# Delta attention with two feed-forward layers: another order of the opening

## The chip, the cores and the metric

The kernel runs on one core of a Trainium2 chip. The metric is device time in microseconds, from launch to the end of the last instruction; several runs of the same program are given by their median. The engines named below are TensorE (PE), VectorE (DVE), ScalarE (ACT), GpSimd (POOL) and SyncE (SP), whose queue issues the DMAs.

## The reference

For 4 batches and 8 heads, a state of 48 x 48 goes through 768 positions by the delta rule: at each position the output is read with q, then the state takes up what v adds to what the state already says of the normalised k, weighted by beta. The result is laid out as 3072 tokens of 384 columns and goes through two feed-forward layers, the first gated (silu), the second with the mish function.

```python
k_n = k / (np.linalg.norm(k, axis=-1, keepdims=True) + 1e-06)
for t in range(S):
    kt, vt, bt = (k_n[:, :, t], v[:, :, t], beta[:, :, t, None])
    y[:, :, t] = np.einsum('bhd,bhde->bhe', q[:, :, t], state)
    v_old = np.einsum('bhde,bhd->bhe', state, kt)
    state = state + bt[:, :, :, None] * np.einsum('bhd,bhe->bhde', kt, vt - v_old)
...
x = x @ w_gate * sigmoid(x @ w_gate) * (x @ w_val) @ w_out
h = x @ w_in;  out = (h * np.tanh(np.log1p(np.exp(h)))) @ w_out
```

## The kernel before

The 768 positions are cut into 24 chunks of 32; three chunks make a step of 384 tokens, and there are eight steps. Within a chunk the recurrence is written as matrix products. A gram of the keys (gram) gives a triangular system of 32 x 32 for each of 24 systems of a step (3 chunks of 8 heads). Its inverse t is found column by column: one instruction multiplies (t_tmp, lines 298 and 366) and one subtracts (t_sys, lines 305 and 373). In the first two steps only the two halves of 16 are solved so, and two small products, the joins (lines 323 and 334), make the missing corner out of them. For a join the solved system has to be turned around: three transpositions on VectorE (lines 311, 312 and 314) write the right half of t, its transposed left half, and the left half of t. Then z = t v (line 413), the output y (lines 392, 445 and 456) and the state's update ds (line 483) follow. In the first step two batches share one matmul of 64 rows, for which some operands are written twice, each copy masked by turn_of: g_wide, t_wide, tT_wide and p_wide.

Beside this TensorE runs the first feed-forward layer on the tokens of the step before: for each of twelve tiles j the products g and v (line 747, nine matmuls each) and then, one tile late, the product x (line 819, nine matmuls). Each of these is a group; a step has 36 of them. The second layer follows when all steps are done.

The weights arrive as 64-bit numbers and are converted on the chip. For a tile of the first layer ScalarE does lines 677 and 679 on raw, VectorE line 700 (f), ScalarE line 716 and VectorE or GpSimd line 720. The tiles of the second layer go back to device memory. The f tiles of the first layer and the raw tiles of the second share two buffers in turn.

Each engine's queue holds the instructions in the order in which the program writes them. Up to the first product of the main loop that order is the table START: a word is a piece of work (ja0 the first half of a join of chunk 0, jb0 its second half, h4 four matmuls that only keep TensorE's clock, P5 five columns of the second step's solve on GpSimd, vs the scaling of v, qw the masked copy of p, b the conversion of a weight tile). A word with > behind it stops after the matmuls; with > ahead of it the rest follows. In the main loop, the attention of the next step and the weight tiles are events with a time in groups, and an event is written out as soon as the groups reach its time. BEGIN says where in a step the attention of step t begins, FILL where the weight tiles of the first layer are converted, LEAD how much earlier they are loaded.

Of the kernel before, what the change touches and what calls it, by code (L numbers as in the profile page):

```python
# [12 lines left out]
AF = mybir.ActivationFunctionType  # L13
ALU = mybir.AluOpType
# [3 lines left out]
NEXT = 1.4  # L18
TURN = 32.6
CHAIN = (0.0, 0.28, 0.58)  # L20
BEGIN = {1:7.8,2:9.5,3:5.5}
STEADY = 4.0
LAST = 33.0
XSAT = (0.1, 1.7, 3.3)
FB = 3
START = """
sq0 sq1 sq2 h12 kq0 kq1 norm kq2 turn0 scale diag s3 wide kq3 s3 kq4 b0 s3 h17 b1 kg5 h10 s6 back0 mr ma ml vs0 clear vs1 vs2 qw0
ja0> h3 >ja0 turn1 jb0> h4 nb >jb0 ns1 z0> >z0 ja1> >ja1 ns1 u0> >u0 jb1> >jb1 ns1 r1> y1 ne >r1 gam1 z1> >z1 scale diag P5 qw1 P4 qw2 P6 ja2> >ja2 u1> d1 >u1 jb2> >jb2 y0 o0> >o0 d1 r2> y2 >r2 d1 z2> >z2 t1 x0> >x0 o1> >o1 t1 >x0 o2> >o2 x1> t1 >x1 >x1 x2> u2> >x2 >x2 d3 done
"""
FILL = (1.2, 2.9)  # L30
W2AT = (4.5, 4.0, 3)
# [4 lines left out]
OPEN = 2  # L36
# [22 lines left out]
def tile_delta_attention_moe_moe(  # L59
# [10 lines left out]
    nc = tc.nc  # L70
    D = 48
    H = k.shape[2] // D
    B, C = 4, 32
# [4 lines left out]
    CH = NCH * H  # L78
    HB = C // 2
# [4 lines left out]
    J1 = w_first.shape[0] // 3  # L84
# [18 lines left out]
    turn_of = const.tile([128, 2], F32, name="turn_of")  # L103
# [70 lines left out]
    tT_nat = lent10[:, 1, 0:C * 32].rearrange("p (a b) -> p a b", b=C)  # L174
# [423 lines left out]
    ev = []  # L598
# [59 lines left out]
    def fetch(u, n=3):  # L658
        if u >= n_prep or quiet and u >= FIRST:
            return  # L660
        open_raw(u)
        for i in range(came_in[u], min(came_in[u] + n, pieces_of(u))):
            src = w_first[3 * u + i] if u < J1 else w_second[2 * (u - J1) + i]
            nc.sync.dma_start(out=raws[u][:, 384 * i:384 * i + 384], in_=src.rearrange("p k f -> p (k f)"))
            came_in[u] += 1

    def conv_begin(u, which=(0, 1)):
        if u >= n_prep:
            return
        fetch(u)  # L670
        raw = raws[u]
        word = raw.bitcast(U32).rearrange("p (f w) -> p f w", w=2)
        top = raw.bitcast(U16).rearrange("p (f w) -> p f w", w=4)

        high = word[:, :, 1].bitcast(F32)
        if 0 in which:
            nc.scalar.activation(out=high, in_=high, func=AF.Prelu, scale=2.0 ** -112, alpha=2.0 ** 32)
        if 1 in which:
            nc.scalar.activation(
                out=word[:, :, 0], in_=top[:, :, 1], func=AF.Identity, scale=2.0 ** -13, bias=floor  # L680
            )
            words_of[u] = word
            begun[0] = max(begun[0], u + 1)
# [22 lines left out]
    def conv_tail(u, n=3):  # L706
        n = min(n, stepped[u] - tailed[u])
        if not n:
            return
        f, first = parts_of[u], tailed[u]  # L710
        if u < J1:
            sl = slice(3 * first, 3 * (first + n))
            if not first:
                w1_open(u)
            f = f[:, 0:1152].rearrange("p (k f) -> p k f", f=128)
            nc.scalar.copy(out=w1h[u][:, sl], in_=f[:, sl])
            for i in range(first, first + n):
                sl = slice(3 * i, 3 * i + 3)
                eng = nc.vector if u < OPEN else nc.gpsimd
                eng.tensor_tensor(out=w1l[u][:, sl], in0=f[:, sl], in1=w1h[u][:, sl], op=ALU.subtract)  # L720
        else:
            for i in range(2):
                nc.sync.dma_start(
                    out=w2d[u - J1][:, 3 * i:3 * i + 3], in_=f[i].rearrange("p (k f) -> p k f", k=3)
                )
        tailed[u] += n
        while ended[0] < n_prep and tailed[ended[0]] == pieces_of(ended[0]):
            ended[0] += 1
# [236 lines left out]

    hold0 = [{} for _ in range(NCH)]

    def widen(out, in_, at_):
        for x in range(2):
            nc.scalar.activation(  # L970
                out=out[:, :, x, at_], in_=in_[:, 0:CH, at_], func=AF.Identity, scale=turn_of[:, x:x + 1]
            )

    words = {
# [11 lines left out]
            )  # L986
            for x in range(2)
        ],
        "mr": lambda n: widen(t_wide, lent_tn, slice(HB, C)),
        "ma": lambda n: widen(tT_wide, tT_nat, slice(0, HB)),  # L990
        "ml": lambda n: [
            nc.gpsimd.tensor_scalar(
                out=t_wide[:, :, x, 0:HB], in0=lent_tn[:, 0:CH, 0:HB], scalar1=turn_of[:, x:x + 1], scalar2=None,
                op0=ALU.mult,
            )
            for x in range(2)
        ],
        "sq": square_sums,
        "norm": lambda n: (nc.vector.transpose(out=gam, in_=n_nat), norms(gam), gammas(0)),
        "turn": turn_g,  # L1000
# [59 lines left out]
    for i in range(SOLVES[2]):  # L1060
        ev.append((SOLVES[0] + SOLVES[1] * i, lambda: solve_next(1, 1, nc.vector)))
    for i, u in enumerate(range(OPEN, J1 + 1)):
        p = FILL[0] + FILL[1] * i
        ev.append((p - 2.0, lambda u=u: u < begun[0] or conv_begin(u, (0,))))
        ev.append((p - 1.0, lambda u=u: u < begun[0] or conv_begin(u, (1,))))
        for _ in range(3):
            ev.append((p - LEAD + _, lambda u=u: fetch(u, 1)))
        ev.append((p, lambda u=u: u < J1 and conv_step(u)))
        ev.append((p + 0.7, lambda u=u: u < J1 and conv_tail(u)))

    def needed(g):

# [157 lines left out]
```

## Time and profile before

| | us |
|---|---|
| median of 3 runs | 1081.23 (1079.38 to 1084.43) |
| profiled execution | 1084.8 |
| its span, first to last instruction | 1082.8 |
| PE busy | 1040.7 (96%) |
| PE weight loads busy | 997.9 (92%) |
| DVE busy | 511.1 (47%) |
| ACT busy | 392.4 (36%) |
| POOL busy | 191.8 (18%) |

[...] Busy shares are means over stages that differ: the opening, the main loop beside the attention, and the second layer. What one stage can give or lose is read from the waits and the clock in that stage. A busy PE is not PE at its peak, since matmuls overlap.

### The profile page before, as it was taken

To read this page: it belongs to the slowest core of one execution; us is meant where nothing else is said; L and a number is where in the kernel's file an instruction comes from. 1 tells how busy PE (TensorE), PEld (TensorE's weight loads), DVE (VectorE), ACT (ScalarE), POOL (GpSimd) and SP (SyncE) were. 2 spreads that over 40 slices of the span, in tenths; PEclk is the share of its full clock that TensorE was granted. 3 is DMA by queue.
4 is the path that set the end of the run, shared out by engine and by line. 5 is a ranking of instruction groups with operands and counts; after the bars stand their busy time and mean duration, and the time that the engine had idled before them with its cause. 6 is when DMAs were issued, how large, how long until landed. Compare 5 with 4: busy or idle time off the path is not lost.

```text
span 1082.8 us, 27944 instructions
## 1 busy us (share of the span) xinstructions
PE 1040.7 (96%) x12310; PEld 997.9 (92%) x12310; DVE 511.1 (47%) x1096; ACT 392.4 (36%) x785; POOL 191.8 (18%) x228
## 2 busy tenths in 40 slices
PE   6988888999999999999999999999999999999998
PEld 6877778998999999999999999999999999999998
DVE  7542787488686685884862244212121212212111
ACT  5355553324324234234232345423333332323232
POOL 2464652122221312221211122000000000000000
PEclk7678998999999999999999999999999999999999
DMA  8144443322414215114010043101010000100000
GB/s 298 33 136 132 160 148 109 117 63 84 140 36 154 72 51 174 44 50 145 25 38 24 9 140 117 59 1 45 16 29 23 23 30 15 37 9 30 1 22 22
DMA packets 37704, 77.41 MB, mean 71 GB/s; under 512 B 4176, under 2 KB 23760, under 8 KB 37584
## 3 DMA queue, kind: packets, MB, share of 16 engines
q1 hardware_dynamic: 37584, 75.65, 21.2%
q8 instruction: 96, 1.57, 0.6%
q14 instruction: 24, 0.20, 0.1%
HBM read 59.90 MB, written 15.73 MB: 70 GB/s over the span
## 4 chain that ended last, share of the span: by engine, by line
PE 79%; DVE 9%; DMA 3%; POOL 3%; ACT 3%; issue 2%; SPq 1%; DVEq 0%; ACTq 0%; POOLq 0%
PE o L747 19%; PE h L747 19%; PE v L747 11%; PE g L747 10%; PE x L819 10%; DVE t_tmp L366 3%; DVE t_sys L373 2%; DMA raw<-in_w_first_dram 2%; PE ds L483 2%; PE y L392 2%; PE ks L392 2%; PE y L456 1%; PE z L420 1%; POOL w1r L720 1%; DVE h L798 1%
## 5 line engine op out<-in xcount | busy, mean ns | idle before, releaser
L1136 DVE TENSOR_TENSOR gl<-gg,gh 128x384 fp32r<-128x384 f32 x128 | 71.5, 559 | 319.2 <-ACT gh L1135 319.2
L804 POOL TENSOR_TENSOR hp<-h,hp 128x384 fp32r<-128x384 f32 x96 | 100.8, 1050 | 437.0 <-ACT hp L803 437.0
L819 PE MATMUL x<-hp,w1r 128*128 128x384 f32 x864 | 172.2, 340 | 2.3 <-ACT hp L803 1.9
L1130 ACT ACTIVATE gg<-h 128x384 f32<-128x384 f32 x128 | 62.9, 492 | 264.8 <-PE h L747 264.8
L819 PEld LDWEIGHTS x<-hp,w1r 128*128 128x128 f32 x864 | 150.1, 189 | 8.2 <-ACT hp L803 2.6
L747 PE MATMUL g<-xh,w1r 128*128 128x384 f32 x576 | 122.7, 346 | 8.0 <-ACT s L790 8.0
L747 PE MATMUL v<-xh,w1r 128*128 128x384 f32 x576 | 118.6, 340 | 6.1 <-DVE h L798 6.1
L803 ACT CAST hp<-h 128x384 fp32r<-128x384 f32 x96 | 49.3, 513 | 177.8 <-DVE h L798 177.7
L747 PEld LDWEIGHTS g<-xh,w1r 128*128 128x128 f32 x576 | 102.7, 192 | 11.4 <-ACT s L790 9.0
L747 PEld LDWEIGHTS v<-xh,w1r 128*128 128x128 f32 x576 | 102.0, 190 | 9.1 <-DVE h L798 8.3
L798 DVE TENSOR_TENSOR h<-s,v 128x384 f32<-128x384 f32 x96 | 52.9, 551 | 76.0 <-PE v L747 66.5
L747 PE MATMUL o<-w2l,gh 128*128 128x384 f32 x240 | 81.2, 338 | 0.0
L747 PE MATMUL o<-w2h,gl 128*128 128x384 f32 x240 | 81.1, 338 | 0.0
L747 PE MATMUL o<-w2h,gh 128*128 128x384 f32 x240 | 81.1, 338 | 0.0
L747 PE MATMUL o<-w2r,gh 128*128 128x384 f32 x288 | 80.4, 335 | 0.0
L373 DVE TENSOR_TENSOR t_sys<-t_sys,t_tmp 128x31 f32<-128x31 f32 (+15 forms) x186 | 77.1, 415 | 6.4
L366 DVE TENSOR_TENSOR t_tmp<-t_sys,g_sys 128x31 f32<-128x31 f32 (+15 forms) x186 | 77.6, 417 | 4.7
L790 ACT ACTIVATE s<-g 128x384 f32<-128x384 f32 x96 | 47.1, 491 | 88.0 <-PE g L747 87.8
L501 DVE TENSOR_TENSOR state<-state,ds 48x384 f32<-48x384 f32 x84 | 42.8, 548 | 56.3 <-PE ds L483 55.9
L747 PE MATMUL v<-xl,w1r 128*128 128x384 f32 x288 | 66.6, 338 | 1.7 <-issue 1.7
L747 PE MATMUL g<-xl,w1r 128*128 128x384 f32 x288 | 68.2, 345 | 0.0
L1135 ACT CAST gh<-gg 128x384 fp32r<-128x384 f32 x128 | 64.6, 505 | 0.7 <-PE o L747 0.7
(146 smaller groups left out, 1648.9 us busy)
## 6 DMA issues: line engine op xcount, KB each, us to landing
raw<-in_w_first_dram SPq DMA_DIRECT2D x36, 384.0 KB, 4.5
raw<-in_w_second_dram SPq DMA_DIRECT2D x32, 384.0 KB, 4.3
kqT<-in_kq_dram SPq DMA_DIRECT2D x23, 512.0 KB, 5.0
w2d<-f SPq DMA_DIRECT2D x32, 192.0 KB, 2.0
w2raw<-w2d SPq DMA_DIRECT2D x16, 384.0 KB, 3.1
v<-in_v_dram SPq DMA_DIRECT2D x24, 192.0 KB, 3.5
x2d<-xs SPq DMA_DIRECT2D x24, 192.0 KB, 1.9
x2raw<-x2d SPq DMA_DIRECT2D x24, 192.0 KB, 2.4
```

Of the source, the lines that this page charges most:

```text
L366: nc.vector.tensor_tensor(out=tmp, in0=t_sys[:, 0:m, j:j + 1].to_broadcast([128, m, n]), in1=g_sys[:, j:j + 1, j + 1:C].to_broadcast([128, ...
L373: nc.vector.tensor_tensor(out=sl, in0=sl, in1=tmp, op=ALU.subtract)
L392: nc.tensor.matmul(out=ps[bs, 2 * p:2 * p + 2], lhsT=kqt[:, p, w, bs], rhs=state[:, b, p], start=not w or p == 0, stop=not w, skip_group_c ...
L747: nc.tensor.matmul(out=ps, lhsT=a, rhs=b, start=start and i == 0, stop=stop and i == len(seq) - 1)
L790: nc.scalar.activation(out=s, in_=ps, func=AF.Silu)
L798: nc.vector.tensor_tensor(out=h, in0=g_t.pop(j), in1=ps, op=ALU.mult)
L803: nc.scalar.copy(out=hh, in_=h)
L804: nc.gpsimd.tensor_tensor(out=hl, in0=h, in1=hh, op=ALU.subtract)
L819: nc.tensor.matmul(out=x2[kk], lhsT=w[j][:, 6 + kk, :], rhs=m, start=j == 0 and i == 0, stop=j == J1 - 1 and i == 2,)
L1130: nc.scalar.activation(out=gg, in_=ps, func=AF.Mish)
L1135: nc.scalar.copy(out=gh, in_=gg)
L1136: nc.vector.tensor_tensor(out=gl, in0=gg, in1=gh, op=ALU.subtract)
```

## The change

The table START gets another order, and some words are split or added.

- The first join comes behind the first two transpositions; the third is written behind the first half of the second join. The join's first half needs only the first transposition and the gram.
- The masked copies of t and of its transpose (words mr, ma, ml) are made for chunk 0 first and for chunks 1 and 2 later. The copies of the left half move from GpSimd to ScalarE.
- The conversion of weight tile 1 (b1) is split into its two instructions (p1, l1), which move behind the second chunk's joins; tile 2's first instruction (p2) comes into the opening.
- On GpSimd v of chunk 0 is scaled first of all, the three masked copies of p come together, and the 15 columns of the second step's solve follow in one piece (P15 for P5, P4 and P6).
- There are three more clock-keeping matmuls behind the first join's first half, and two new ones behind the second chunk's first half.
- In the plan, step 2's attention begins at group 11.0 of its step instead of 9.5, and the first tile of the second layer is handled at 33.5 instead of 30.2. The second tile of that layer gets a load of its own at 35.0.

```diff
--- before.py
+++ after.py
@@ -18,14 +18,14 @@
 NEXT = 1.4
 TURN = 32.6
 CHAIN = (0.0, 0.28, 0.58)
-BEGIN = {1:7.8,2:9.5,3:5.5}
+BEGIN = {1:7.8,2:11.0,3:5.5}
 STEADY = 4.0
 LAST = 33.0
 XSAT = (0.1, 1.7, 3.3)
 FB = 3
 START = """
-sq0 sq1 sq2 h12 kq0 kq1 norm kq2 turn0 scale diag s3 wide kq3 s3 kq4 b0 s3 h17 b1 kg5 h10 s6 back0 mr ma ml vs0 clear vs1 vs2 qw0
...
+sq0 sq1 sq2 h12 kq0 kq1 norm vs0 kq2 turn0 scale diag s3 wide kq3 s3 kq4 b0 s3 h17 kg5 h10 s6 backa0
+ja0> h6 >ja0 ma0 jb0> backc0 mr0 ml0 h4 clear vs1 vs2 qw0 qw1 qw2 >jb0 ma1 turn1 z0> >z0 nb ja1> >ja1 h2 ns1 u0> mr1 >u0 ml1 ns1 jb1> >jb1 p1 r1> y1 >r1 ns1 ne z1> >z1 gam1 ja2> >ja2 scale diag P15 u1> l1 >u1 jb2> p2 >jb2 y0 o0> >o0 d1 r2> y2 >r2 d1 z2> >z2 d1 x0> t1 >x0 o1> >o1 t1 >x0 o2> >o2 x1> t1 >x1 >x1 x2> u2> >x2 >x2 d3 done
 """
 FILL = (1.2, 2.9)
 W2AT = (4.5, 4.0, 3)
@@ -965,10 +965,11 @@

     hold0 = [{} for _ in range(NCH)]

-    def widen(out, in_, at_):
+    def widen(out, in_, at_, rest):
+        sl = slice(H, CH) if rest else slice(0, H)
         for x in range(2):
             nc.scalar.activation(
-                out=out[:, :, x, at_], in_=in_[:, 0:CH, at_], func=AF.Identity, scale=turn_of[:, x:x + 1]
+                out=out[:, sl, x, at_], in_=in_[:, sl, at_], func=AF.Identity, scale=turn_of[:, x:x + 1]
             )

     words = {
@@ -986,15 +987,11 @@
             )
             for x in range(2)
         ],
-        "mr": lambda n: widen(t_wide, lent_tn, slice(HB, C)),
-        "ma": lambda n: widen(tT_wide, tT_nat, slice(0, HB)),
-        "ml": lambda n: [
-            nc.gpsimd.tensor_scalar(
-                out=t_wide[:, :, x, 0:HB], in0=lent_tn[:, 0:CH, 0:HB], scalar1=turn_of[:, x:x + 1], scalar2=None,
-                op0=ALU.mult,
-            )
-            for x in range(2)
-        ],
+        "mr": lambda n: widen(t_wide, lent_tn, slice(HB, C), n),
+        "ma": lambda n: widen(tT_wide, tT_nat, slice(0, HB), n),
+        "ml": lambda n: widen(t_wide, lent_tn, slice(0, HB), n),
+        "p": lambda n: conv_begin(n, (0,)),
+        "l": lambda n: conv_begin(n, (1,)),
         "sq": square_sums,
         "norm": lambda n: (nc.vector.transpose(out=gam, in_=n_nat), norms(gam), gammas(0)),
         "turn": turn_g,
@@ -1060,13 +1057,16 @@
     for i in range(SOLVES[2]):
         ev.append((SOLVES[0] + SOLVES[1] * i, lambda: solve_next(1, 1, nc.vector)))
     for i, u in enumerate(range(OPEN, J1 + 1)):
-        p = FILL[0] + FILL[1] * i
-        ev.append((p - 2.0, lambda u=u: u < begun[0] or conv_begin(u, (0,))))
+        p = FILL[0] + FILL[1] * i if u < J1 else 33.5
+        if u > OPEN:
+            ev.append((p - 2.0, lambda u=u: u < begun[0] or conv_begin(u, (0,))))
         ev.append((p - 1.0, lambda u=u: u < begun[0] or conv_begin(u, (1,))))
         for _ in range(3):
             ev.append((p - LEAD + _, lambda u=u: fetch(u, 1)))
         ev.append((p, lambda u=u: u < J1 and conv_step(u)))
         ev.append((p + 0.7, lambda u=u: u < J1 and conv_tail(u)))
+
+    ev.append((35.0, lambda: fetch(J1 + 1)))

     def needed(g):
```

The ScalarE queue in the opening, before, from the conversion of weight tile 0 (raw_173; raw_177 is tile 1) to the first z. Here lent_134 holds the second step's gram and the transposed t, lent_136 is t, lent_138 and lent_139 are t_wide and tT_wide:

```order
L679 ACTIVATE raw_173<-raw_173,floor 128x1152
L677 ACTIVATE raw_177<-raw_177 128x1152
L679 ACTIVATE raw_177<-raw_177,floor 128x1152
L543 COPY lent_134<-gram 128x4x32 x2
L970 ACTIVATE lent_138<-lent_136,turn_of 128x24x16 x2
L970 ACTIVATE lent_139<-lent_134,turn_of 128x24x16 x2
L353 ACTIVATE lent_135<-join,upper 128x128
L428 ACTIVATE z_s<-z,turn_of 128x384
```

And now:

```order
L679 ACTIVATE raw_173<-raw_173,floor 128x1152
L543 COPY lent_134<-gram 128x4x32 x2
L353 ACTIVATE lent_135<-join,upper 128x128
L971 ACTIVATE lent_139<-lent_134,turn_of 128x8x16 x2
L971 ACTIVATE lent_138<-lent_136,turn_of 128x8x16 x4
L971 ACTIVATE lent_139<-lent_134,turn_of 128x16x16 x2
L428 ACTIVATE z_s<-z,turn_of 128x384
L433 COPY lent_138<-z 128x384
L353 ACTIVATE lent_135<-join,upper 128x128
L971 ACTIVATE lent_138<-lent_136,turn_of 128x16x16 x2
L497 COPY state<-ds 48x4x2x48 x2
L971 ACTIVATE lent_138<-lent_136,turn_of 128x16x16 x2
```

Tile 1's conversion has left the place ahead of the gram's copy and the join's, and four masked copies on this engine have become twelve smaller ones, two pairs of them around the state's copy (line 497). The tile's first half follows behind them.

The GpSimd queue from the scaling of v (v_84 to v_86 are chunks 0 to 2) through the masked copies of p (p_92 to p_94); one piece of the difference:

```order
-L992 TENSOR_SCALAR lent_138<-lent_136,turn_of 128x24x16 x2
 L356 TENSOR_TENSOR v_84<-v_84,n_nat 128x384
-L1013 MEMSET t_sys 128x1024
+L1010 MEMSET t_sys 128x1024
 L356 TENSOR_TENSOR v_85<-v_85,n_nat 128x384
 L356 TENSOR_TENSOR v_86<-v_86,n_nat 128x384
-L979 TENSOR_TENSOR lent_140<-p_92,lent_140 128x512
+L980 TENSOR_TENSOR lent_140<-p_92,lent_140 128x512
+L980 TENSOR_TENSOR lent_140<-p_93,lent_140 128x512
+L980 TENSOR_TENSOR lent_140<-p_94,lent_140 128x512
 L298 TENSOR_TENSOR t_tmp<-t_sys,g_sys 128x30
```

The masked copies of t are gone from here, and the three of p now stand ahead of the solve's first column.

The SyncE queue where the second layer's first weights are loaded (raw_2041 is the last tile of the first layer), before:

```order
L664 DMA raw_2041<-in_w_first_dram 128x384 x3
L664 DMA raw<-in_w_second_dram 128x384 x2
L161 DMA v_86<-in_v_dram 128x384
L168 DMA kqT_87<-in_kq_dram 128x1024
L161 DMA k_83<-in_k_dram 128x384
L768 DMA x2d_126<-xs 128x384 x3
L723 DMA w2d_110<-f 128x384 x2
L664 DMA raw<-in_w_second_dram 128x384 x4
```

And now, where the last tile is raw_2052:

```order
L664 DMA raw_2052<-in_w_first_dram 128x384 x3
L161 DMA v_86<-in_v_dram 128x384
L664 DMA raw<-in_w_second_dram 128x384
L168 DMA kqT_87<-in_kq_dram 128x1024
L664 DMA raw<-in_w_second_dram 128x384
L161 DMA k_83<-in_k_dram 128x384
L664 DMA raw<-in_w_second_dram 128x384 x2
L768 DMA x2d_126<-xs 128x384 x3
L723 DMA w2d_110<-f 128x384 x2
L664 DMA raw<-in_w_second_dram 128x384 x2
```

The first second-layer tile's two loads have moved behind v and between kqT and k, and the second tile's two loads stand ahead of the stores of x2d instead of behind those of w2d.

## Rows read from the trace of the kernel before

**Rows 1.** chain of waits, 0 to 130 us: start, length, what

```profile
12.92 9.39 DMA raw<-in_w_first_dram
...
23.71 1.23 ACT raw L679
...
25.46 1.95 PE join L323 x32
...
41.30 1.90 PE z L413 x32
```

**Rows 2.** timeline, 20 to 31 us: start, length, engine, line, operation, idle before it

```profile
21.89 2.02 PE L941 MATMUL heat<-cold 128*128 128x384 f32 x10
...
22.57 1.30 DVE L311 STREAM_TRANSPOSE lent<-t_sys 128x512 f32<-128x512 f32 x1
...
23.73 1.09 DVE L312 STREAM_TRANSPOSE lent<-t_sys 128x512 f32<-128x512 f32 x1
...
25.19 2.13 ACT L970 ACTIVATE lent<-lent,turn_of 128x384 f32<-128x384 f32 x4
...
27.45 0.37 ACT L353 ACTIVATE lent<-join,upper 128x128 f32<-128x128 f32 x1
...
30.65 0.61 DVE L346 SCALAR_TENSOR_TENSOR lent<-join,turn_of,lent 128x128 f32<-128x128 f32 x2 [2.80 <-PE join L323]
```

**Rows 3.** half-microsecond stretches: PE, PEld, DVE, ACT, POOL busy, granted clock, DMA, GB/s

```profile
26.00:26.50 0.50, 0.50 (x14) 0.50 (x12) 0.50 (x1) 0.50 (x2) 0.50 (x1) 0.80 0.00 0
...
43.00:43.50 0.50, 0.50 (x15) 0.50 (x14) 0.00 (x0) 0.21 (x1) 0.00 (x0) 0.64 0.17 33
```

**Rows 4.** timeline, 31 to 50 us

```profile
31.49 1.27 POOL L979 TENSOR_TENSOR lent<-p,lent 128x512 f32<-128x512 f32 x1
...
31.61 1.19 DVE L261 SCALAR_TENSOR_TENSOR t_tmp<-t_tmp 128x32 f32<-128x32 f32 x1
...
43.90 0.62 DVE L429 TENSOR_SCALAR z_s<-z,turn_of 128x384 f32<-128x384 f32 x1 [2.33 <-ACT z_s L428]
...
45.37 0.40 POOL L298 TENSOR_TENSOR t_tmp<-t_sys,g_sys 128x30 f32<-128x30 f32 x1 [12.61 <-DVE t_sys L280]
...
45.39 1.08 PE L323 MATMUL join<-lent,lent 64*64 64x16 f32 x32
...
45.72 0.97 ACT L497 COPY state<-ds 48x384 f32<-48x384 f32 x2 [0.41 <-PE ds L483]
...
48.90 1.14 PE L413 MATMUL z<-v,lent 64*64 64x48 f32 x32
```

**Rows 5.** timeline, 57 to 72 us

```profile
57.12 1.95 PE L445 MATMUL y<-lent,lent 64*64 64x48 f32 x32 [4.62 <-POOL lent L979]
...
61.98 0.27 POOL L305 TENSOR_TENSOR t_sys<-t_sys,t_tmp 128x30 f32<-128x30 f32 x1
...
62.60 0.56 DVE L521 TENSOR_TENSOR xl<-xt,xh 128x384 fp32r<-128x384 f32 x1 [1.50 <-ACT xh L519]
...
70.31 1.29 DVE L311 STREAM_TRANSPOSE t_nat<-t_sys 128x512 f32<-128x512 f32 x1
```

**Rows 6.** timeline, 147 to 152 us

```profile
147.90 1.25 ACT L677 ACTIVATE raw<-raw 128x1152 f32<-128x1152 f32 x1 [1.43 <-DMA raw<-in_w_first_dram]
...
151.72 1.58 PE L747 MATMUL g<-xh,w1r 128*128 128x384 f32 x6 [3.38 <-ACT s L790]
```

**Rows 7.** timeline, 178 to 185 us

```profile
178.06 1.82 SPq L664 DMA_DIRECT2D raw<-in_w_second_dram  x4
...
184.82 2.29 PE L747 MATMUL g<-xh,w1r 128*128 128x384 f32 x6 [4.17 <-ACT s L790]
```

**Rows 8.** chain of waits, 184 to 196 us

```profile
184.82 3.25 PE g L747 x9
...
193.96 1.56 PE g L747 x9
```

**Rows 9.** a stretch of 20 us, columns as in rows 3

```profile
240.00:260.00 20.00, 17.54 (x103) 16.78 (x102) 18.38 (x46) 5.75 (x13) 3.23 (x3) 1.00 0.10 35
```

More of the change, by code (lines that the diff above doesn't have):

```diff
@@ L26 @@
 START = """
-sq0 sq1 sq2 h12 kq0 kq1 norm kq2 turn0 scale diag s3 wide kq3 s3 kq4 b0 s3 h17 b1 kg5 h10 s6 back0 mr ma ml vs0 clear vs1 vs2 qw0
-ja0> h3 >ja0 turn1 jb0> h4 nb >jb0 ns1 z0> >z0 ja1> >ja1 ns1 u0> >u0 jb1> >jb1 ns1 r1> y1 ne >r1 gam1 z1> >z1 scale diag P5 qw1 P4 qw2 P6 ja2> >ja2 u1> d1 >u1 jb2> >jb2 y0 o0> >o0 d1 r2> y2 >r2 d1 z2> >z2 t1 x0> >x0 o1> >o1 t1 >x0 o2> >o2 x1> t1 >x1 >x1 x2> u2> >x2 >x2 d3 done
+sq0 sq1 sq2 h12 kq0 kq1 norm vs0 kq2 turn0 scale diag s3 wide kq3 s3 kq4 b0 s3 h17 kg5 h10 s6 backa0
+ja0> h6 >ja0 ma0 jb0> backc0 mr0 ml0 h4 clear vs1 vs2 qw0 qw1 qw2 >jb0 ma1 turn1 z0> >z0 nb ja1> >ja1 h2 ns1 u0> mr1 >u0 ml1 ns1 jb1> >jb1 p1 r1> y1 >r1 ns1 ne z1> >z1 gam1 ja2> >ja2 scale diag P15 u1> l1 >u1 jb2> p2 >jb2 y0 o0> >o0 d1 r2> y2 >r2 d1 z2> >z2 d1 x0> t1 >x0 o1> >o1 t1 >x0 o2> >o2 x1> t1 >x1 >x1 x2> u2> >x2 >x2 d3 done
 """
```

## The prediction

> **What bounds the kernel now.** I began with the chain of waits over the first 130 us, because everything the change touches, apart from three numbers of the plan, lies ahead of the first feed-forward product. Read it from the top [rows 1]: a DMA of first-layer weights, then ScalarE's conversion of the second weight tile (raw, lines 677 and 679), and only then the first join on TensorE at 25.46. All twelve steps of the chain from that join to the product z of the second chunk, 25.46 to 43.20, are TensorE's own. So two things hold the opening: a weight conversion that the attention does not need, and TensorE itself.
>
> Second, the timeline around the first join [rows 2]. The transposition that the join needs (line 311) ended at 23.87. The ten clock-keeping matmuls ended at 23.91. TensorE then sat idle 1.55 us. Third, the granted clock in half microseconds [rows 3]: it left 1.00 at about 26.3, shortly after that idle time, and came back only at about 43.2. Hence 32 join matmuls take 1.95 us in rows 1 and 1.08 us in rows 4. [...]
>
> Fourth, the end of the opening [rows 5]: TensorE waited 4.62 us at the third chunk's output (y, line 445) for GpSimd's masked copy of p, which stands in GpSimd's queue between steps of the second step's solve. Last, two long waits in the steady part: 3.38 us ahead of 151.72 [rows 6] and 4.17 us ahead of 184.82 [rows 7], both behind a ScalarE queue whose head was a weight conversion waiting for its DMA.
>
> **The change part by part**, against the profiled execution (1084.8 us, span 1082.8, so 2.0 us lie around the span; the median of the runs is 1081.23, and I carry the gain over to that).
>
> *The first join.* ScalarE no longer converts weight tile 1 (2.5 us) ahead of the join's operand. After tile 0's conversion it copies the gram at about 22.1, so the join waits for line 311 alone and starts at 23.9: 1.5 us gained, and no idle time behind the ten warm matmuls. The copies masked by turn_of are now made for the first eight of 24 systems first: 128 columns each, which the trace does not show. The nearest rows are 0.37 us (128 columns from PSUM) and 0.53 us (a quarter of the 2.13 for 384 columns) [rows 2]; I take 0.37, whose size is the same, and 0.45 for those of 256 columns.
>
> *To the first z.* At the full clock: join 23.9 + 1.08 = 25.0; its copy 0.37 and two masked copies 0.74 make 26.2; the six warm matmuls, 0.2 each by the ten in rows 2, run beside them. Second join to 27.4, VectorE's two additions 0.61 [rows 2], so z starts at 28.2. Its v is ready, since v's scaling now comes in GpSimd's idle time near 12 us. GpSimd's three masked copies, 1.27 us each [rows 4], lie at about 28.4 to 32.2. One of them in the old place held a VectorE instruction on 32 columns for 1.19 us [rows 4]; now VectorE's norm steps are there instead of its state copies, which read PSUM, so I cost this at nothing, up to 1.3 us if the state copy is caught behind it. [...]
>
> *To z of the second chunk.* z 1.14 [rows 4]; z_s on ScalarE and VectorE, 0.6 each by VectorE's row; ds of 32 matmuls, about 1.0 by the join and z of rows 4: 31.8. ScalarE's two state copies (0.97) stand behind a join's copy and two more masked copies (0.37 + 0.9, begun at about 31.1): 33.4. ks and y at 0.9 each, z 1.14, ScalarE's 0.6: VectorE's z_s starts at 37.1 instead of 43.90 [rows 4]. That is 6.8 us gained. Bounds: 1.5 if the clock falls as before; TensorE's 17.7 us of chain halved, 8.9, and the 1.5 make 10.4.
>
> *To the last xl.* Now ScalarE's queue gets worse. One conversion of 1.25 us stands ahead of the second state copy, another ahead of the first y copy, which the third y's bank waits for. Both lie on the path: I count 1.6 us lost, so z of the third chunk ends at 44.8 instead of 50.04. From there the old way to the end of the last xl (63.16) took 13.1 us. The 4.62 us wait for the masked copy goes, since all three are done by 32.2, and the 32 matmuls of that y run in 1.14 instead of 1.95. That leaves 7.6: 52.4. The opening ends **10.7 us** earlier. What is late next is xt on its bank, which waits for xl and was there before too. GpSimd's solve, now in one piece, starts behind VectorE's diagonal at about 39.6. Before it ran 45.37 to 62.25, 16.9 us, with two masked copies inside, so 14.4 now: 54.0. VectorE's transposition of its result, at 70.31 before [rows 5], would come at 59.6, so 5.6 us are left.
>
> *Does it carry?* The main loop's start is tied to the conversion that follows the last xl on VectorE, then ScalarE and GpSimd; none of it is tied to an absolute time. The put-off loads are released by z of the third chunk, 5.2 us earlier, against a main loop 10.7 us earlier: 5.5 us less cover. I count nothing, and 2 us as the other end if the fourth tile's load is late.
>
> *The wait at 184.82.* The four loads of raw at 178.06 [rows 7] could not be issued before VectorE had used the previous tile: raw tiles and f tiles share two buffers. The change loads the first second-layer tile after the last f tile, and the second at group 35 into the other buffer. Then its conversion finds the data there. The 4.17 us go, and the slow clock behind them: nine matmuls 3.25 instead of 1.56, 1.69 us [rows 8], and six more by the same ratio 1.1: **7.0 us** in all. Bounds: 2.8 (VectorE takes the wait's place) and 7.0.
>
> *The wait at 151.72.* The second-layer loads no longer run beside the last first-layer tile. I estimate its landing 1.6 us earlier, and perhaps no slow stretch: **2.0 us**, bounds 0 and 4.
>
> *The plan.* Step 2's attention begins at 11.0 instead of 9.5, so step 3's solve on VectorE starts one group later and must end at the same place. VectorE is busy 18.38 of 20 us there [rows 9], so about a group's time is paid: **1.5 us** lost, bounds 0 and 3.
>
> Sum: 10.7 + 7.0 + 2.0 - 1.5 = 18.2 us. Against the profiled run that is 1066.6; against the median, 1063.0.
>
> **The rivals.** *A, the clock falls in the opening in spite of the extra matmuls.* For: joins with 16 columns kept company with every low stretch. Against: they ran at 1.00 after 43.2 [rows 4]. About eight path steps cost 0.8 more: gain 12, 1069.
>
> *B, VectorE takes the place of the weight waits.* For: it is the fullest engine beside TensorE [rows 9], and it used the old waits. The 4.17 us come back, the second term is nothing and the plan costs 3: 10.7 + 2.8 - 3 = 10.5, 1071.
>
> *C, ScalarE's longer queue binds the opening.* Twelve small masked copies at 0.53 and three conversions all on the path give back some 6.5 us: 1070. Against: most of them stand where it waits for TensorE.
>
> [...]
>
> **How the numbers follow.** Forecast 0.60, A 0.17, B 0.13, C 0.06, D 0.04. The likeliest case alone spans 1058 to 1068; with A, B and C the 80% range is 1055 to 1074. What can be told from no change here is 0.5%, 5.4 us. Faster: everything but D and a sliver of B and C, 0.93; same 0.03; slower 0.04.
>
> **What would show it.** The first join near 23.9 with no idle time ahead of it; a granted clock of 1.00 from 20 to about 48; the third y not waiting for GpSimd; the last xl near 52; no wait of over 2 us ahead of the gate product at the start of the second step. It would be wrong if the clock rows show 0.50 at 26 to 43 again, if ScalarE's state copies start after 34, or if VectorE's h holds TensorE for over 4 us between 150 and 260.

## The result, and the profile after

The changed kernel took **1067.33 us** (median of 4 runs, 1064.47 to 1069.65), the kernel before 1082.83 beside it: ratio 0.986, 95% interval 0.982 to 0.990. Run once more later, unaltered, it took 1067.57 (6 runs, 1065.22 to 1072.70; ratio 0.987, 0.984 to 0.989). The forecast was 1063.0, with a range of 1055 to 1074. The profiled run took 1066.75 with a span of 1065.0, 18.05 us under the profiled run of before; TensorE's mean granted clock, a share of its full speed, was 0.986 in it and 0.972 before. So for this one pair of profiled runs the sum of the prediction, 18.2, came out almost exactly, but not by its own terms: that closeness is luck. The medians differ by 15.5, and the profiled run of before was one of the longest of its kernel. One way to see this is to follow one product of the main loop, h on VectorE (line 798, 96 of them), through both traces. Starts in us:

| h product | before | after | gain by then | the same kernel again | gain by then |
|---|---|---|---|---|---|
| 1st (the opening lies ahead) | 68.69 | 63.14 | 5.55 | 60.52 | 8.17 |
| 8th | 135.71 | 125.97 | 9.74 | 124.93 | 10.78 |
| 13th (behind the wait at 151.72) | 171.92 | 161.13 | 10.79 | 159.33 | 12.59 |
| 96th (behind that at 184.82 and the plan) | 673.22 | 655.31 | 17.91 | 653.65 | 19.57 |

Predicted were 10.7 for the opening, nothing up to the 8th, 2.0 for the wait at 151.72 and 7.0 less 1.5 behind it. Measured in the first profile: 5.55, 4.19, 1.05 and 7.12; in the second: 8.17, 2.61, 1.81 and 6.98.

**The opening.** The timeline of the changed kernel from 22 to 31 us, TensorE, VectorE and ScalarE, answers to [rows 2]:

```profile
22.86 1.23 DVE L311 STREAM_TRANSPOSE lent<-t_sys 128x512 f32<-128x512 f32 x1
...
24.39 1.94 PE L323 MATMUL join<-lent,lent 64*64 64x16 f32 x32
26.26 1.32 PE L941 MATMUL heat<-cold 128*128 128x384 f32 x6
27.51 1.11 PE L323 MATMUL join<-lent,lent 64*64 64x16 f32 x32
...
26.38 0.37 ACT L353 ACTIVATE lent<-join,upper 128x128 f32<-128x128 f32 x1 [3.17 <-PE join L323]
26.64 2.65 ACT L971 ACTIVATE lent<-lent,turn_of 128x128 f32<-128x128 f32 x8
```

The join starts without an idle time ahead of it, 1.07 us earlier than at 25.46 in [rows 1]; line 311 ends at 24.09, where 23.9 was forecast. The masked copies cost 2.65 / 8 = 0.33 each (0.37 was taken). But the first half of the join takes 1.94 us and the second 1.11, at one and the same granted clock of 1.00. The next view has half-microsecond stretches of this kernel: TensorE busy, granted clock, DMA share, GB/s. It answers to [rows 3]:

```profile
32.00:32.50 0.50, 0.50 (x11) 1.00 0.00 0
32.50:33.00 0.50, 0.50 (x3) 0.61 0.00 0
...
39.00:39.50 0.50, 0.50 (x14) 0.57 0.00 0
```

The clock left 1.00 at about 32.6 instead of 26.3, and came back at about 39.4; before, it came back at about 43.4, a little later than the forecast's 43.2. TensorE had had no gap of over 0.15 us since 22.4. Further on, answering to [rows 4], then the last part of the opening, answering to [rows 5]:

```profile
33.25 1.53 PE L483 MATMUL ds<-z_s,k 64*48 64x96 f32 x32
...
41.07 0.62 DVE L429 TENSOR_SCALAR z_s<-z,turn_of 128x384 f32<-128x384 f32 x1 [1.52 <-ACT z_s L428]
...
42.40 1.34 ACT L679 ACTIVATE raw<-raw,floor 128x1152 uint32<-128x1152 uint16 x1
43.64 0.96 ACT L497 COPY state<-ds 48x384 f32<-48x384 f32 x2
44.62 1.31 ACT L677 ACTIVATE raw<-raw 128x1152 f32<-128x1152 f32 x1
...
46.48 0.87 PE L392 MATMUL y<-state,kqT 128*32 128x96 f32 x32 [0.98 <-ACT y L465]
47.28 1.14 PE L413 MATMUL z<-v,lent 64*64 64x48 f32 x32
```

```profile
28.47 3.75 POOL L980 TENSOR_TENSOR lent<-p,lent 128x512 f32<-128x512 f32 x3
...
48.83 2.07 PE L445 MATMUL y<-lent,lent 64*64 64x48 f32 x64
...
52.44 0.69 DVE L720 TENSOR_TENSOR w1r<-f,w1r 128x384 fp32r<-128x384 f32 x1 [0.52 <-ACT w1r L716]
53.05 0.55 DVE L521 TENSOR_TENSOR xl<-xt,xh 128x384 fp32r<-128x384 f32 x1
...
53.74 0.87 PE L514 MATMUL xt<-ident,y 128*128 128x128 f32 x3 [2.84 <-DVE xl L521]
...
57.22 0.56 DVE L521 TENSOR_TENSOR xl<-xt,xh 128x384 fp32r<-128x384 f32 x1 [1.51 <-ACT xh L519]
```

The third y follows the second at once (64 matmuls in 2.07 us): GpSimd's three masked copies were done at 32.22, and the 4.62 us of [rows 5] are gone. In their place TensorE waits 2.84 us for xl. VectorE comes to xl only after two parts of a weight tile (line 720), each behind ScalarE's cast. Before, that work ran while TensorE waited for GpSimd (52.50 to 57.12):

```profile
53.47 0.56 DVE L720 TENSOR_TENSOR w1r<-f,w1r 128x384 fp32r<-128x384 f32 x1 [1.31 <-ACT w1r L716]
53.95 0.55 DVE L521 TENSOR_TENSOR xl<-xt,xh 128x384 fp32r<-128x384 f32 x1
```

The last xl ends at 57.78 instead of 63.16; 52.4 was forecast.

**The first step.** Before, the clock fell once more here. Stretches of the kernel before, columns as above, and then of the changed one:

```profile
80.00:84.00 4.00, 2.29 (x73) 1.00 0.73 208
84.00:95.00 11.00, 8.48 (x188) 0.53 0.41 146
```

```profile
76.00:86.00 10.00, 7.49 (x248) 1.00 0.30 115
86.00:97.00 11.00, 10.17 (x266) 1.00 0.54 163
```

TensorE's longest waits in that place were hardly shorter after the change. First before, then after:

```profile
82.49 0.33 PE L747 MATMUL v<-xl,w1r 128*128 128x384 f32 x1 [1.71 <-issue]
85.57 1.04 PE L334 MATMUL join<-lent,lent 32*32 32x16 f32 x60 [1.44 <-DVE p L548]
```

```profile
76.29 0.79 PE L747 MATMUL v<-xh,w1r 128*128 128x384 f32 x3 [1.70 <-issue]
81.14 1.29 PE L334 MATMUL join<-lent,lent 32*32 32x16 f32 x128 [2.22 <-DVE p L548]
```

Yet the clock stayed at 1.00, and 4.4 us were gained between the third and the fourth h. Nothing of this was in the forecast, and it does not belong to the program alone: in the second profile of the same kernel the clock fell at about 67 and 81, and 2.9 us were gained there.

**The two weight waits.** The wait of 3.38 us in [rows 6] has shrunk to 2.31, and ScalarE's conversion ahead of it no longer waits for its DMA. In the timeline of the changed kernel:

```profile
137.12 1.26 ACT L677 ACTIVATE raw<-raw 128x1152 f32<-128x1152 f32 x1 [0.31 <-POOL hp L804]
...
140.96 1.57 PE L747 MATMUL g<-xh,w1r 128*128 128x384 f32 x6 [2.31 <-ACT s L790]
```

The 4.17 us of [rows 7] are gone, and nothing took their place: from 158 to 230 us TensorE waits for no other engine. Blocks of nine matmuls there take 1.56 us, where the first in [rows 8] took 3.25:

```profile
165.80 0.93 SPq L664 DMA_DIRECT2D raw<-in_w_second_dram  x2
...
168.13 1.72 PE L819 MATMUL x<-hp,w1r 128*128 128x384 f32 x9
169.69 1.20 PE L747 MATMUL g<-xh,w1r 128*128 128x384 f32 x6
170.73 0.68 PE L747 MATMUL g<-xl,w1r 128*128 128x384 f32 x3
```

### The profile page after: what moved, and what is told of

It is laid out like the page before. It is cut to its first block, busy times and chain, and to the rows that moved or that the text cites. A ratio compares the mean times of both kernels' runs of the same rounds, so it can differ in the third digit from the quotient of the medians.

```text
span 1065.0 us, 27970 instructions
## 1 busy us (share of the span) xinstructions
PE 1031.4 (97%) x12315; PEld 988.8 (93%) x12315; DVE 508.4 (48%) x1096; ACT 395.3 (37%) x793; POOL 188.3 (18%) x226
## 4 chain that ended last, share of the span: by engine, by line
PE 82%; DVE 7%; DMA 3%; ACT 3%; POOL 2%; issue 2%; SPq 1%; DVEq 0%; ACTq 0%; POOLq 0%
PE o L747 19%; PE h L747 19%; PE v L747 11%; PE x L819 11%; PE g L747 11%; DVE t_tmp L366 2%; DMA raw<-in_w_first_dram 2%; DVE t_sys L373 2%; PE y L392 2%; PE ds L483 2%; PE y L456 1%; PE ks L392 1%; POOL w1r L720 1%; PE z L420 1%; PE gram L532 1%
```

## The experiments

Twelve kernels, in four groups that each shared a chip with the kernel before. Medians; the last columns are of the profiled run: start of the first join and of the last z, end of the last xl, mean granted clock from 24 to 50 us.

| kernel | us (runs) | ratio to before, 95% | join | last z | last xl | clock |
|---|---|---|---|---|---|---|
| before | 1081 to 1083 | | 25.46 | 48.90 | 63.16 | 0.67 |
| after | 1067.33 (4) | 0.982 to 0.990 | 24.39 | 47.28 | 57.78 | 0.87 |
| 1 opening alone | 1076.02 (12) | 0.994 to 0.998 | 24.72 | 45.39 | 55.84 | 1.00 |
| 2 plan alone | 1072.72 (6) | 0.989 to 0.993 | 25.77 | 47.49 | 57.36 | 0.87 |
| 3 columns | 1068.29 (4) | 0.985 to 0.989 | 24.62 | 45.73 | 56.22 | 0.93 |
| 4 old heat | 1070.73 (6) | 0.987 to 0.991 | 24.41 | 48.45 | 58.97 | 0.74 |
| 5 copies between | 1071.50 (5) | 0.989 to 0.991 | 24.44 | 47.40 | 60.90 | 0.87 |
| 6 conversions behind | 1069.23 (6) | 0.986 to 0.990 | 24.21 | 44.20 | 54.39 | 1.00 |
| 7 old number of the plan | 1074.39 (6) | 0.987 to 0.994 | 24.35 | 52.62 | 63.38 | 0.56 |
| 8 no early load | 1074.84 (6) | 0.991 to 0.995 | 25.18 | 50.03 | 60.54 | 0.74 |
| 9 after again | 1067.57 (6) | 0.984 to 0.989 | 24.10 | 44.66 | 55.17 | 1.00 |
| 10 three orders | 1067.55 (4) | 0.983 to 0.987 | 24.90 | 46.06 | 56.39 | 0.87 |
| 11 three and heat | 1066.26 (4) | 0.982 to 0.986 | 24.87 | 44.25 | 54.60 | 1.00 |
| 12 heat in waits | 1063.81 (6) | 0.980 to 0.986 | 25.08 | 44.45 | 54.11 | 1.00 |

**1 and 2, the two halves.** Kernel 1 is the change without its plan:

```diff
-BEGIN = {1:7.8,2:11.0,3:5.5}
+BEGIN = {1:7.8,2:9.5,3:5.5}
-        p = FILL[0] + FILL[1] * i if u < J1 else 33.5
+        p = FILL[0] + FILL[1] * i
-    ev.append((35.0, lambda: fetch(J1 + 1)))
```

> The changed opening with the old plan (step 2's attention at 9.5, the second layer's first tile at 30.2, no early load of its second tile). My theory: the opening itself is worth 5.5 us at the end of the last xl (57.8 against 63.2), whatever the clock then does between 72 and 97 us is worth 0 to 4 more, and the two waits at the end of the first step (3.4 and 4.2 us) come back as they were: 1073 to 1078, ratio to before 0.991 to 0.995. Rival: the higher clock of the opening carries the whole gain and the plan gives nothing: about 1067, ratio 0.986. In the trace the gate product at the start of the second step waits over 4 us by my theory, under 2 by the rival.

Kernel 2 is the kernel before with these three lines alone changed the other way.

> The old opening with the new plan. My theory: about 1.6 us from the last first-layer tile's earlier landing, 7 to 8.5 from the early load of the second layer's second tile, 1 lost on step 3's solve: 8 to 9 us, 1074, ratio 0.991 to 0.993, and the last xl still near 63. Rival: VectorE takes the place of the removed waits because the old opening leaves it the same work, and the plan is worth 3 us or less: 1080, ratio above 0.996.

The medians gained 6.2 and 9.5 us; together 15.7, against 15.5 for the whole. The parts add up. With the old plan, kernel 1 has the wait at the start of the second step as before:

```profile
172.46 2.29 PE L747 MATMUL g<-xh,w1r 128*128 128x384 f32 x6 [4.39 <-ACT s L790]
```

By h products, kernel 2 gained 7.4 us behind the 13th, kernel 1 gained 0.15. The predicted 10.7 and 7.5 stand against 6.2 and 9.5. Kernel 2 also has the old opening, and yet its last xl ended at 57.36, not at 63.16, since its clock held until 40 us. In its trace:

```profile
52.17 1.14 PE L445 MATMUL y<-lent,lent 64*64 64x48 f32 x32 [2.00 <-POOL lent L979]
...
55.35 0.90 PE L514 MATMUL xt<-ident,y 128*128 128x128 f32 x3 [1.57 <-DVE xl L521]
```

The wait for GpSimd was 2.00 us there instead of 4.62. So of what one profiled opening gains or loses, over 5 us can be the clock and the waits that follow from it, and not the order of the work. With a mean clock of 0.87 from 24 to 50 us the last xl ended at 57.36 in the old order (kernel 2) and at 57.78 in the new one.

The single runs say the same of the opening's 6.2 us. Kernel 1's four runs with a mean clock of 0.972 to 0.978 took 1080.6 to 1083.9 us, just as the nine runs of the kernel before at these clocks did. Its other eight, at 0.983 to 0.989, took 1072.6 to 1076.5. Kernel 2's six runs, at 0.977 to 0.984, took 1067.9 to 1074.3, where the kernel before took 1078.6 to 1082.7 at 0.977 to 0.983. So the plan gains at an equal clock, while most of what the new opening gains comes with a higher clock (0.982 in the mean of kernel 1's runs, 0.978 before). Whether the order, the clock-keeping matmuls or the shorter waits raise it, these two kernels can't tell.

**3, the join's operand in columns.** The first half of the join reads its stationary operand with a step of 32 words; here the words lie next to each other.

```diff
-    g_wide = lent8[:, 0:64 * 32].rearrange("p (a b) -> p a b", b=32)
+    g_wide = lent8[:, 0:64 * 32].rearrange("p (b a) -> p a b", b=32)
```

> The changed kernel, with g_wide laid out so that the 64 numbers of one system lie side by side: the stationary operand of a join's first half is then read without a stride. In the changed kernel the first halves took 1.92 to 1.94 us at a granted clock of 1.00, the second halves 1.05 to 1.11. My theory: it is the stride of the stationary operand, so the first halves fall to 1.0 to 1.1 us, the first z starts 0.8 us earlier, the last xl 1 to 2 us earlier, and the time falls by 1 to 2 us against the changed kernel (1065 to 1066, ratio 0.984). Rival: the first halves are slow because their operands' writers end only just before, or because the clock shown is not the one that these matmuls get: they stay at 1.9 us and nothing changes.

```profile
24.62 1.11 PE L323 MATMUL join<-lent,lent 64*64 64x16 f32 x32
...
34.88 1.51 PE L392 MATMUL ks<-state,kqT 128*32 128x96 f32 x32 [1.49 <-DVE state L499]
```

1.11 instead of 1.94 us, so it was the step through memory, not the clock, that made the first halves long. With the step, the clock hardly matters: 30 matmuls of a first half took 1.78 us at 0.50 before and 1.79 at 1.00 after the change.

```profile
33.74 1.78 PE L323 MATMUL join<-lent,lent 64*64 64x16 f32 x30
```

```profile
40.18 1.79 PE L323 MATMUL join<-lent,lent 64*64 64x16 f32 x30
```

The last xl came 1.56 us earlier, but ks waited 1.49 us for VectorE's state copy, which stands behind norm steps, and the clock fell at other places of the first step. One of these norm steps, on 32 columns, took 1.32 us, to 32.68; in the changed kernel it took 0.30, to 32.27, where GpSimd's masked copies ended at 32.22. The prediction had bounded that by 1.3 and counted nothing.

```profile
31.36 1.32 DVE L250 TENSOR_SCALAR t_tmp<-g_sys 128x32 f32<-128x32 f32 x1
```

No gain in time is shown: 1068.29, where 1065 to 1066 was expected.

**4, the old number of clock-keeping matmuls** (three instead of six behind the first half, none instead of two ahead of ds):

```diff
-ja0> h6 >ja0
+ja0> h3 >ja0
->ja1 h2 ns1
+>ja1 ns1
```

> The changed kernel with the old number of clock-keeping matmuls: three instead of six behind the first join's first half, none instead of two behind the second chunk's. My theory: the clock fell at 32.7 us although TensorE never stood still from 22 us on, so the extra matmuls do not keep it, and the two of the second chunk stand in the way of ds, which started at 33.3 while its operand was ready at 32.1: without them ds starts 0.4 to 0.9 us earlier and the last xl 0.5 us earlier or the same, time within 1 us of the changed kernel. Rival: they do keep the clock; without them it falls by 27 us as it did before, the eight steps behind cost 0.8 us each at most, and the last xl comes 3 to 6 us later (1070 to 1073).

The clock fell at 27.2 and came back at 40.8, and the last xl ended 1.19 us later. The median is 3.4 us above that of the changed kernel, with overlapping intervals. The time lies in the rival's range, the last xl does not. That is a hint that these matmuls help, and experiments 5 to 9 show why one profile can't prove it.

**5, GpSimd's masked copies between the steps of its solve, as before:**

```diff
-qw0 qw1 qw2 >jb0
+qw0 >jb0
-scale diag P15 u1>
+scale diag P5 qw1 P4 qw2 P6 u1>
```

> The changed kernel with GpSimd's second and third masked copies of p back in their old places, between steps of its solve; everything else as after the change. After the change the third y (L445) found its operand ready, where before it waited 4.62 us for the third copy. If that wait belongs to the copies' places: the wait for GpSimd is back, of 2 to 5 us, the last xl ends at 60 to 62 instead of 57.78, and the time is 1069 to 1072. Rival, that the state copies of the third chunk, not GpSimd, would now end that wait: the last xl moves by under 0.5 us, and the time stays within 2 us of 1067.3. GpSimd's solve ends near 60 in both cases, ahead of its transposition at 64.8.

```profile
54.84 1.94 PE L445 MATMUL y<-lent,lent 64*64 64x48 f32 x32 [4.59 <-POOL lent L980]
```

The wait is back, the time within the first expectation, and against the first profile of the changed kernel, with the same clock of 0.87, the last xl ends 3.1 us later, not 4.6: 1.5 of the wait covered the work for xl.

**6, ScalarE's conversions behind the copies that TensorE waits for:**

```diff
-u1> l1 >u1 jb2> p2 >jb2 y0 o0> >o0 d1 r2> y2 >r2 d1
+u1> >u1 l1 jb2> >jb2 y0 o0> >o0 d1 r2> y2 >r2 p2 d1
```

> The changed kernel with two conversions of weight tiles on ScalarE moved: the one ahead of the third chunk's state copy (L679 at 42.40, 1.34 us) goes behind it, the one ahead of the y copy (L677 at 44.62, 1.31 us) behind the copy of the third y. If these two lie on the path, as the prediction has it (1.6 us lost), z of the third chunk ends 1.6 to 2.6 us earlier than 48.42, the last xl near 55.5 to 56, and the opening is 2 us shorter. Rival, that TensorE or VectorE holds the end by then: z of the third chunk earlier by under 0.5 us. What the time does: 1065 if the gain carries, 1066 to 1070 if the clock falls at other places of the first step, as it did with the joins in columns, where 1.56 us at the last xl were lost again by 100 us.

Beside kernel 9, whose clock was also 1.00 up to 50, the last z starts 0.46 us earlier and the last xl ends 0.78 earlier. This is the two conversions' price, half of the 1.6 in the forecast; at z it is under 0.5, as the rival had it. The time, 1069.23, isn't better: the clock fell at 75 to 85.5 in its first step.

**7 and 8, the plan's number and the early load.** Kernel 7 changes `2:11.0` back to `2:9.5`; kernel 8 takes out the line `ev.append((35.0, lambda: fetch(J1 + 1)))`.

> The changed kernel with the one number of the plan back, step 2's attention begun at 9.5 instead of 11.0. The prediction has the new number as a loss of 1.5 us (before to after, step 3's stretch lost 1.1): then this is 1065.8 to 1066.3, with the opening and the wait at 184.82 as after the change. Rival: with the weight waits gone, VectorE binds the start of step 2, and an attention begun earlier there puts its products ahead of what the feed-forward waits for: a wait of TensorE for VectorE of 1 to 3 us between 185 and 215, and 1069 to 1070.

> The changed kernel without the early load of the second tile of second-layer weights (the fetch at group 35). If the wait at the start of step 2 was behind the raw tile's two buffers, as the prediction has it: TensorE waits about 4 us again ahead of the gate product there, behind ScalarE's queue, the granted clock falls to 0.50 for some 5 us after it, the gain between the last h of step 1 and those of step 2 (8.5 us in the changed kernel) is gone but for 0 to 2 us, and the time is 1074 to 1075.5. Rival, that the later conversion and the order of the first tile's load make the difference: a wait under 2 us, a clock that stays at 1.00, and 1067 to 1069.

Kernel 7's median met neither expectation: its times go from 1065.6 at a mean clock of 0.990 to 1078.9 at 0.980, and in the profiled one the clock fell at 26.5 and stayed low until 54.5. Behind the 13th h, where the number acts, it gained 6.6 us on before, the changed kernel 7.1 (7.0 in its second profile). The rows that differ are these, of kernel 7 and then of the changed kernel:

```profile
246.30 1.32 PE L747 MATMUL v<-xh,w1r 128*128 128x384 f32 x6 [1.06 <-DVE h L798]
```

```profile
237.88 1.31 PE L747 MATMUL v<-xh,w1r 128*128 128x384 f32 x6 [0.30 <-DVE h L798]
```

So the rival has the direction and the place is later, 240 us: an attention begun earlier puts VectorE in the way by 0.8 us. The new number costs nothing in these traces; they give 0.4 to 0.5 us in its favour. The trace of before has a wait of 1.04 us at this place too.

Kernel 8's time lies in its first range, but with a clock of 0.74 in the opening; behind the 13th h it still gained 2.4 us, so the early load carries 4.7 of the 7.1. The wait is back, 2.98 us instead of the 4.17 of [rows 7], and the clock falls with it (timeline, then stretches as above):

```profile
178.53 1.97 PE L747 MATMUL g<-xh,w1r 128*128 128x384 f32 x6 [2.98 <-ACT s L790]
```

```profile
174.00:178.00 4.00, 1.55 (x9) 1.00 0.82 323
178.00:182.00 4.00, 3.47 (x12) 0.62 0.00 0
```

**9, the changed kernel again**, no line altered.

> The changed kernel once more, not a line altered. Up to its 26th us, its instructions in the opening are those of four other profiled runs here (with the plan alone put back, with the copies of p between, with the old number of the plan, without the early load), and the clock fell in these at 50.5, 32.0, 26.5 and 28.5 us. If the moment at which the clock falls in the opening is no matter of the program, this run shows it at yet another moment than 32.5, its last xl ends between 55 and 63, and its times spread over 8 us or more, longer where the mean clock is lower. Rival: the moment belongs to the program and the parts that these kernels undid moved it: then it falls at 32.5 again, the last xl ends within 0.5 of 57.78, and the times lie within 1064 to 1070.

The clock held until 50 this time, and the last xl ended at 55.17 instead of 57.78. In kernels 1, 5, 7 and 8, which give TensorE the same instructions in the opening, the fall came at 50.5, 32.0, 26.5 and 28.5 (read in half microseconds). The moment is no matter of the program alone. The six times span 7.5 us, a little less than the 8 expected, and follow the mean granted clock: 1065.2 to 1065.9 at 0.989 to 0.994, 1069.2 to 1072.7 at 0.982 to 0.984.

**10 and 11, three orders together, and with more heat.** Kernel 10 has the edits of 3 and 6 and the state copy ahead of the norm steps; kernel 11 adds six heat matmuls:

```diff
-ns1 u0> mr1 >u0 ml1 ns1 jb1>
+u0> mr1 >u0 ml1 ns1 ns1 jb1>
# kernel 11 as well
-h6 >ja0 ... h2 u0> ... >jb1 p1
+h7 >ja0 ... h4 u0> ... >jb1 h3 p1
```

> The changed kernel with three orders of the opening altered together: the first operand of the joins in columns that lie next to each other, the two conversions of weight tiles behind the copies that TensorE waits for, and VectorE's state copy of the first chunk ahead of its norm steps instead of between them (in the run with columns alone it came at 33.71, and TensorE waited 1.49 us for it). What the opening gains at the full clock: 1.6 by the columns, 1.5 to 2 by the conversions, 0.8 by the state copy: the last xl at 53 if the clock holds, 55 if it falls near 33. The time 1064 to 1066 if that carries to the end; the rival, that what the opening gains is lost again to a clock that falls in the first step, says 1067 to 1070.

> The kernel with the three orders together, and six clock-keeping matmuls more in the opening: one behind the first half of the first join, two behind that of the second, three behind its second half. They cost 0.2 us each at the full clock where TensorE has no wait, 0.6 in all beyond the waits that they fill. If such matmuls hold the clock, it stays at 1.00 until the weights' products begin (past 50), the last xl ends near 54, and the time is 1063 to 1065 with a narrow spread. Rival, that the fall comes whatever these matmuls do: it falls between 26 and 40 in this profile, or the mean clock and the times spread as without them, and the time is 0 to 1 us above the kernel with the three orders alone.

The state copy starts at 32.78 instead of 33.71 and ks waits 0.28. In kernel 10 the clock fell at 38.5, and its time is that of the changed kernel, as the rival said. In kernel 11 it held to 50, but its time lies above the 1063 to 1065 expected; its four runs lie within 1.7 us, those of kernel 9 within 7.5. So few runs make the narrower spread a hint only.

**12, heat in the waits for xl**, on top of kernel 11:

```diff
->o2 x1> t1 >x1 >x1 x2>
+>o2 H8 x1> t1 >x1 >x1 H4 x2>
-nc.tensor.matmul(out=ps, lhsT=xh[:, 0, 0:128], rhs=xh[:, 0, :], start=True, stop=True)
+nc.tensor.matmul(out=ps, lhsT=cold[:, 0:128], rhs=cold, start=True, stop=True)
```

> The kernel with the three orders and more heat, and twelve matmuls on zeros more: eight ahead of the second chunk's transposition of the output (xt, L514), where TensorE was idle 2.69 us from 47.86 in that kernel, and four ahead of the third's, idle 1.16. In every kernel of this study the clock fell within 5 us of these two waits, and 6.8 us or more ran at 0.50 there. If the idle time brings that fall, it is gone: the granted clock stays at 1.00 from 50 to 58, ds and the first products take 0.88 and 1.16 instead of 1.53 and 2.29, the loop starts up to 3.4 us earlier and the time is 1063 to 1064.5. Rival, that the fall has another cause, or that the xl of the first tile, not TensorE, holds the loop: it falls between 48 and 60 as before, the last xl moves by under 1 us, and the time is 1066 to 1067.

The stretch from 50 to 60 us, kernel 11 and then kernel 12 (the columns of the stretches above), and kernel 12's timeline:

```profile
50.00:60.00 10.00, 8.29 (x61) 0.66 0.56 212
```

```profile
50.00:60.00 10.00, 7.23 (x67) 1.00 0.52 200
```

```profile
47.99 1.68 PE L946 MATMUL heat<-cold 128*128 128x384 f32 x8
50.77 0.52 PE L514 MATMUL xt<-ident,y 128*128 128x128 f32 x3 [1.09 <-DVE xl L521]
51.04 0.96 PE L946 MATMUL heat<-cold 128*128 128x384 f32 x4
...
58.69 1.31 PE L747 MATMUL g<-xh,w1r 128*128 128x384 f32 x6 [1.55 <-ACT s L790]
```

The low clock that each other kernel has there (0.65 to 0.80 in the mean from 50 to 60) is gone; the clock fell at 65.8 and came back at 69.2. The first products run at the full clock, but then wait 1.55 us for the next weight tile, so the 1st h comes only 0.4 us earlier than in kernel 11. The rest is kept further on: 12.43 us gained on before at the fourth h, against 9.71. The time is 1063.81 (1061.56 to 1070.68), 3.5 us below the changed kernel's; its interval (0.980 to 0.986) and that of kernel 9 (0.984 to 0.989) overlap a little, so that it beats the changed kernel is likely and not shown.

## Why the prediction was right, and where it was not

*The direction and the range held; the sum met the first profile by luck.* Both halves of the change gain, and add up (experiments 1 and 2). The plan's gain is shown by its mechanism (experiment 8). The opening's is shown as a whole, and GpSimd's copies as one part of it (experiment 5); most of it comes with a higher clock, whose cause stays open. The median, 1067.33, lies nearer to rival A's 1069 than to 1063.0.

*The first join: right in kind.* No conversion and no idle time ahead of it; 24.39 for 23.9.

*To z of the third chunk: mis-sized.* Forecast 20.9 us from the start of the first join to the end of that z; 24.03 in the first profile, 21.70 in the second. The 2.3 between them is the clock, rival A, which was given 0.17: it falls in the opening in some executions and not in others. (That joins kept company with every low stretch does not hold even before: it was low from 53.6 to 67.3 without one.) The first profile shows two of the forecast's own signs of being wrong, the clock at 0.50 from 32.6 to 39.4 and ScalarE's state copies at 34.88. The remaining 0.8 is the sum's own: the step "join 23.9 + 1.08" took the row of a second half for a first half. It read the 1.95 of [rows 1] as the slow clock, although the clock was 1.00 for the first 0.8 us of it. In kernel 9 the first halves of the first two chunks took 1.94 and 1.93, and ds starts 8.6 us behind the first join's start; the sum has 6.9. Of these 1.7 us, 0.9 came back: the conversions cost about 0.5 up to there (kernel 6) instead of 1.6.

*To the last xl: mis-sized.* "The old way less 4.62 less 0.81" gave 7.6 us behind z; both profiles show 9.4. The wait went, as said, and kernel 5 brought it back. But xt, named as late next and priced at nothing, takes 1.8 back: with TensorE's wait gone, the weight tile's parts on VectorE and ScalarE stand ahead of xl.

These three make the missing 5.4 us: 0.5, 3.1 and 1.8. What filled the gap in this profile, the clock that didn't fall at 84, was not in the sum.

*The wait at 184.82: right.* 7.0 forecast for the wait and the slow stretch behind it, 6.6 with the old number of the plan, 7.1 with the new; 4.7 of it is the early load (kernel 8). Rival B is out: VectorE did not take the wait's place.

*The plan: wrong.* "About a group's time is paid, 1.5 us" supposed that VectorE binds there because it is busy 18.38 of 20 us [rows 9]. Busy is not bound: TensorE waited for VectorE's h once there, 1.06 us with the old number and 0.30 with the new, so the number gained a little, if anything.

*The wait at 151.72: not shown.* 2.0 forecast; from the 8th to the 13th h, 1.8 in kernel 9 and 1.05 in the first profile, where the clock fell at 141.8. But kernel 1, with the old plan, has a wait of 2.30 there, like the changed kernel's 2.31. Over all profiles with the second layer's first tile at 33.5 the gain is 1.1 to 1.8 where the clock held behind the wait (five) and -0.1 to 1.05 where it fell (seven). So the later loads of that tile are not shown to be the cause.

*Rivals C and D.* ScalarE's conversions lie on the path with 0.5 to 0.8 us, not 6.5. D, given 0.04, was a slower kernel whose clock stays low far into the first step. It did not stay low there: 1.00 in the mean from 60 to 100, and 0.91 in kernel 9.

## What to carry to other kernels

A duration belongs to an operation with its operands' layout (1.94 or 1.11 us for the join's first half): before a row prices another instruction, compare how each reads memory, not only its shape. When a wait goes, write down what other engines did during it; here that work became the next wait (2.84 us for xl). And where the clock falls at other moments in each execution, compare kernels stretch by stretch at the same granted clock, or by many runs.

## What the runs showed of the hardware

- 32 matmuls of 16 columns took 1.94 us with a stationary operand read at a step of 128 bytes (changed kernel) and 1.11 with one in a row (kernels 3 and 10); the clock was 1.00 in the changed kernel and in kernel 10. With the step, 30 of them took the same at a clock of 0.50 (1.78) and of 1.00 (1.79).
- The clock fell at 32.6 with no gap of over 0.15 us on TensorE since 22.4, and stayed at 1.00 through waits of 1.70 and 2.22 us. The same TensorE instructions saw it fall at 26.5, 28.5, 32.0, 32.5 and, in two executions, past 50: here the moment of the fall varied by 24 us.
- Twelve matmuls on zeros in two waits of 2.69 and 1.16 us went with a clock of 1.00 from 50 to 60 us, 0.66 without them; it fell at 65.8 instead. One profile each.
- Two VectorE instructions on 32 columns ended within 0.05 us of GpSimd's masked copies beside them. Line 261 took 1.19 us before, to 32.80, where the copy ended at 32.76; with none beside it, at 35.35, it took 0.19. Line 250 took 0.30 in the changed kernel, to 32.27, where the copies ended at 32.22. It took 1.32 in kernel 3, 1.12 in kernel 11 and 0.47 in kernel 9. Line 429, which reads z from PSUM, took 0.62 beside the copies (at 31.43 in the changed kernel) and 0.62 without (at 41.07).
